# Folding a per-channel scale and shift into the weights and the relu, and normalising all heads at once, in a fused attention and MLP kernel

## The chip, the cores and the metric

The kernel runs on one core of one Trainium2 chip. The metric is the device time of one execution in microseconds (us). A core has five engines that run side by side, each with its own list of instructions in fixed order: TensorE (PE) multiplies matrices out of SBUF into PSUM, VectorE (DVE) and ScalarE (ACT) work elementwise on both memories, GpSimd (POOL) works elementwise on SBUF, and SyncE (SP) issues most of the DMA transfers. They wait for each other through semaphores. The profile counts a weight load of TensorE as an engine of its own, PEld.

## The reference

```python
# attention: batch 4, 8 heads, 768 positions, head size 64; 4 sink keys and a window of 128
scores = q @ k.T / sqrt(64)
keep = is_sink | in_window
a = exp(where(keep, scores, -1e9) - max); a = a / sum(a)
x = (a @ v)                           # laid out as [4, 768, 512]
# residual MLP with affine steps, d_model 512, hidden 2048
a1 = alpha1 * x + beta1
tok = einsum('ts,bsd->btd', w_tok, a1)
u = x + lam * tok
a2 = alpha2 * u + beta2
ch = relu(a2 @ w_ch1) @ w_ch2
out = u + lam * ch
```

Inputs and output are float32; the matrix products are done in float16 with float32 sums.

## The kernel before

The four batches pass one after the other through the same stages, and the attention of the next batch is woven into the MLP of the present one.

Attention. `load_qk`, `trans`: q and k of two heads are cast to float16 and transposed into `qkT`, by TensorE for batches 0 and 1, by the transposing DMA for batches 2 and 3. `scores` computes, for each block j of 128 keys, the scores of the queries in blocks j and j+1, for four heads in one buffer of kind S (two PSUM banks, 1024 columns in all); two of these exist, and one block takes both. ACT takes the exponential into `E`, DVE or POOL masks it. `sinks` does the same for the four sink keys, into `es`. `pv` multiplies `E` with the values, for a block r of 128 queries and a half G of four heads. Each value row has a 1 as its 65th element, so that the 65th column of the result is the sum of the weights. `norm` in `pv` takes the reciprocal of that column and multiplies (L850 and L851). The result of a `pv` stands in a buffer of kind d, one PSUM bank; four of these exist, and the MLP uses them as well. For blocks 2 to 4 of batches 2 and 3 (`EARLY`) the sink part is computed together with the scores of the next block, as two matmuls of 64 rows that run side by side (L711); else it is one matmul of 128 rows for each half (L818).

MLP. On the attention result, POOL and DVE apply alpha1 and beta1 (`xh`; lam is folded into both). `tok` multiplies with the transposed w_tok (L956); DVE adds it to x, which gives u (L963); ACT or POOL casts it to `u16`. u is then transposed: in batch 0 by TensorE (`uTp`, L997), in the others by the transposing DMA (`uTx`, L1015). `affine` applies alpha2 and beta2 to the transposed u, where they are per-partition scalars, in four pieces of 384 columns for each half `chk` of the positions (L980 on ACT, L982 on DVE). `mlp1` computes the hidden layer, fi by fi: four matmuls of 384 columns (L1036), then the relu, on ACT (L1042) or DVE (L1044), into `hT`. For batch 0, `mlp2` does the second product (`ch`, L1221). For batches 1 to 3 it is done by a Strassen scheme with seven products: `h_sums` adds and subtracts quarters of `hT` on DVE (S1 to S4), `w2_sums` those of w_ch2, and `prod` multiplies (P1 to P7, L1153) and adds the results to u (L1166).

What sets the order: nothing runs when it is written. Every piece is added to a plan as a task, with a priority, the engines that can do it with the planner's own cost figure for each, the tasks that it needs, and the buffers that it uses. `Plan.run` simulates the machine and always takes the task that can start first; buffers are given out in that simulation, and where TensorE would stand idle in the first microseconds it puts in multiplications of zeros (`idle`)[...]. The instructions are then written in that order. `TURNS` is a list of seeds by which the priorities are varied before the plan is made. The order is therefore fixed when the kernel is built, and on the chip each engine works through its list.

In the profile, casts and copies have one line for all uses (L356 on ACT, L358 on DVE and POOL).

Of the kernel before, what the change touches and what calls it, by code (L numbers as in the profile page):

```python
# [111 lines left out]
class Plan:  # L112
# [19 lines left out]
    def run(self, prio):  # L132
# [35 lines left out]
        def pick():  # L168
            best = None
            spare = {k: sorted(h for h, x in zip(homes[k], busy[k]) if not x) for k in homes}  # L170
            for r, i in open_:
                at = ready[i]
                if best is not None and at > best[0]:
                    continue
                t = tasks[i]
                asked = {}
                for b in t.uses:
                    if b.home is None:
                        asked[b.kind] = asked.get(b.kind, 0) + 1
                if any(len(spare[k]) < n for k, n in asked.items()):  # L180
                    continue
                at = max([at] + [spare[k][n - 1] for k, n in asked.items()])
                own = None
                for e in t.engs:
                    at_e = max(free[e], at)
                    if e == POOL or (e == DVE and t.port):
                        at_e = max(at_e, port)
                    key = (at_e + FW * t.engs[e], at_e, r, at_e + t.engs[e], i, e)
                    if own is None or key < own:
                        own = key  # L190
                if best is None or own[1:] < best:
                    best = own[1:]
            return best
# [52 lines left out]
    def emit(self, turns):  # L246

        prio = [t.prio for t in self.tasks]
        for seed in turns:
            prio = shuffle(prio, seed)  # L250
        for t, e, start, stop, idle in self.run(prio):
            t.at = (e, start, stop)
            if idle:
                self.fill[1](self.pools["d"][0].tile(
                    [128, 512], FP32, tag=f"d_{idle[0]}", bufs=1, name=f"idle{t.i}"), idle[1])
            for b in t.uses:
                if b.t is None:
                    pool, shape, dtype = self.pools[b.kind]
                    b.t = pool.tile(b.shape or shape, b.dtype or dtype,
                                    tag=f"{b.kind}_{b.home}", bufs=1, name=b.name)  # L260
            t.fn(e)

# [17 lines left out]
def kernel(  # L280
# [51 lines left out]
        "rec": (sb, [P, 4, 1], FP32),  # L332
        "u16": (sb, [P, DM], FP16),
        "uT": (sb, [P, NC, S], FP16),
        "hT": (sb, [P, NF, NTOK], FP16),
# [32 lines left out]
    rsum = const.tile([P, NR], FP32, name="rsum")  # L368
    ab_row = sb.tile([2 * NC, P], FP32, tag="pt_2", bufs=1, name="ab_row")
# [39 lines left out]
    gates = sb.tile([1, 32], FP16, tag="pt_1", bufs=1, name="gates")  # L409
# [7 lines left out]
    TURNS = (13523, 134113, 50022, 128275, 136711, 187603, 125671, 100730, 14946, 163131, 178432, 158827, 183776, 137680, 153375, 26742, 367527, 307353, 376563, 212018, 255075, 397706, 218147, 375675, 393913, 224567, 207692, 352780, 243076, 346008)  # L417
# [164 lines left out]
    EARLY = (2, 3, 4)  # L582
# [107 lines left out]
    def scores(p, b, j, Gs, bias=False):  # L690
# [44 lines left out]
        if b > 1 and j:  # L735
            qk = qk + [done["S", b, j - 1, 0]]
        if early:
            cost += 115
            qk = qk + [done["vs", b, None], done["es", b, 0]]
            more = [es[b]] + [pvb[b, r, G] for G in range(2)]  # L740
        a = add(p, {PE: cost}, mm, qk + [done["bias"]], [o] + [u[3] for u in units] + more, mode="row")
        for G, hps, n, pS, eT in units:
# [8 lines left out]
            if not bias:  # L751
# [12 lines left out]
                if b and j:  # L764
                    c[POOL] = 2 * (150 + n * w * 0.9)
# [43 lines left out]
    def pv(p, b, r, G):  # L809
        early = (b, r, G) in pvb  # L810
        po = pvb[b, r, G] if early else Buf("d", [P, 4, D1], FP32, f"pv{b}_{r}_{G}")
        parts = [(r - 1, P)] * (r > 0) + [(r, 0)]
        Es = [E[b, j, G] for j, _ in parts]

        def mm(e):
            if r >= 2 and not early:
                g = slice(64 * G, 64 * G + 64) if b == 0 else slice(0, P)
                nc.tensor.matmul(  # L818
                    po.t, es[b].t[g, (r - 2) * P : (r - 1) * P], vs[g, 4 * G : 4 * G + 4, :],
                    start=True, stop=False)  # L820
            for hl in range(4):
                h = 4 * G + hl
                i, e_ = hl // 2, hl % 2
                for n, ((j, c), (eT, off)) in enumerate(zip(parts, Es)):
                    nc.tensor.matmul(  # L825
                        po.t[:, hl, :], eT.t[:, e_, off + i, c : c + P], vf[j][:, h, :],
                        start=(r < 2 and n == 0),
                        stop=(n == len(parts) - 1 and (r < 2 or hl == 3)))

        after = [t for j, _ in parts for t in done["E", b, j, G]]  # L830
# [4 lines left out]
        uses = [po] + list(dict.fromkeys(eT for eT, _ in Es))  # L835
        if early:
            after.append(done["S", b, r + 1, 0 if r + 1 < NR - 1 else None])
        elif r >= 2:
            after += [done["vs", b, None if b else G], done["es", b, G if b == 0 else 0]]
            uses.append(es[b])  # L840
        a = add(p, {PE: 245 if early else (130, 245, 355)[min(r, 2)]}, mm, after, uses)
        done["pv", b, r, G] = a
        if G == 0:
            x[b, r] = Buf("x", None, None, f"x{b}_{r}")
            xh[b, r] = Buf("xh", None, None, f"xh{b}_{r}")
# [3 lines left out]
        def norm(e):  # L849
            nc.vector.reciprocal(rec.t, po.t[:, :, D:D1])  # L850
            nc.vector.tensor_mul(  # L851
                bx.t[:, 4 * G : 4 * G + 4, :], po.t[:, :, 0:D], rec.t.to_broadcast([P, 4, D]))

        a = done["x", b, r, G] = add(p + 0.1, {DVE: 640}, norm, [a], [po, rec, bx])
# [10 lines left out]
        elif G == 1:  # L865
# [8 lines left out]
            a = add(p + 0.3, {POOL: 1350}, mul, [a, done["x", b, r, 0], done["la1"]], [bx, bt], port=True)  # L874
# [58 lines left out]
    def cast_w2(p, i):  # L933
        for a in range(4 * i, 4 * i + 4):
            src = wst[f"w2_{a - a % 2}"]
            done["w2", a] = add(
                p, {DVE: 980, POOL: 1400},
# [71 lines left out]
    def uTx(p, b, ti):  # L1009
# [4 lines left out]
        done["uTd", b, ti] = add(  # L1014
# [3 lines left out]
        if ti % 3 < 2:  # L1018
            return
        chk = ti // 3  # L1020
        for c in range(NC):
            o = (c, slice(chk * NTOK, (chk + 1) * NTOK))
            done["uT", b, chk, c] = add(
                p + 0.1 + 0.01 * c, {DVE: 380, ACT: 700},
                lambda e, c=c, o=o: affine(e, bo.t[:, o[0], o[1]], bo.t[:, o[0], o[1]], c),
                [done["uTd", b, 3 * chk + i] for i in range(3)] + [done["ab2"]], [bo])

    def mlp1(p, b, chk, fi):
        if fi == 0:
            hT[b, chk] = Buf("hT", None, None, f"hT{b}_{chk}")  # L1030
        bh, bu = hT[b, chk], uT[b, 0]
        ph = Buf("d", [P, NTOK], FP32, f"h{b}_{chk}_{fi}")

        def mm(e):
            for c in range(NC):
                nc.tensor.matmul(  # L1036
                    ph.t, w1f[:, c, fi * P : (fi + 1) * P],
                    bu.t[:, c, chk * NTOK : (chk + 1) * NTOK], start=(c == 0), stop=(c == NC - 1))

        def relu(e):  # L1040
            if e == ACT:
                nc.scalar.activation(bh.t[:, fi, :], ph.t, AF.Relu)  # L1042
            else:
                nc.vector.tensor_scalar_max(bh.t[:, fi, :], ph.t, 0.0)  # L1044

        a = add(p, {PE: 4 * 161}, mm,
                [done["uT", b, chk, c] for c in range(NC)] + [done["w1", fi // 4]],
                [ph, bu])
        done["h", b, chk, fi] = add(p + 0.1, {ACT: 493, DVE: 556}, relu, [a], [ph, bh])
# [7 lines left out]
    def w2_sums(p):  # L1057

        for g in range(HF // 2):
# [5 lines left out]
            def sub(o, i0, i1, after, n_):  # L1065
# [3 lines left out]
                return add(p + 4 * g + n_, {DVE: 420, POOL: 1400}, f_, after, [bw], port=True)  # L1069
# [8 lines left out]
    def h_sums(p, b, what):  # L1078
# [6 lines left out]
        def s2(g, f):  # L1085
            return own[g].t if own else h0.t[:, f]
# [3 lines left out]
        for g in range(2):  # L1090
# [3 lines left out]
                "S3": lambda e, f=f, g=g: nc.vector.tensor_sub(hs[g].t, h0.t[:, f], h1.t[:, f]),  # L1094
                "S1": lambda e, f=f, k_=k_: nc.vector.tensor_add(h1.t[:, f], h1.t[:, f], h1.t[:, k_]),
                "S2": lambda e, f=f, g=g: nc.vector.tensor_sub(s2(g, f), h1.t[:, f], h0.t[:, f]),
                "S4": lambda e, f=f, k_=k_, g=g: nc.vector.tensor_sub(h0.t[:, k_], h0.t[:, k_], s2(g, f)),
# [12 lines left out]
            done[what, b, g] = add(p + 0.1 * g, {DVE: 880}, made, after, uses, port=True)  # L1110
# [6 lines left out]
    def prod(p, b, what, nt):  # L1117
# [46 lines left out]
        def plus(p, bx, cols, more):  # L1164
# [3 lines left out]
            return add(p, {DVE: 400}, f_, [a, u_] + more, [pc, bx])  # L1168
# [13 lines left out]
        elif what == "P6":  # L1182
# [3 lines left out]
            u = add(p + 0.1, {DVE: 400}, u2, [a, done["read", b, "P1", nt]], [pc, bt])  # L1186
# [9 lines left out]
            done["U12", b, nt] = add(p + 0.3, {POOL: 760, DVE: 400}, ot, [u, done["u16", b, nt]], [bt, top], port=True)  # L1196
# [109 lines left out]
    for b in range(B):  # L1306
# [54 lines left out]
        if b + 1 == STRASSEN[0]:  # L1361
            w2_sums(w0 + ns + PAR["w2s"])
        if b + 1 < B:
# [30 lines left out]
    plan.emit(TURNS)  # L1394
# [35 lines left out]
```

The softmax here doesn't subtract the row's maximum and nothing guards it: scores larger than these inputs give would overflow.

## Time and profile before

| what | value |
| --- | --- |
| time, median of 3 runs | 256.96 us (256.52 to 257.1) |
| span of the profiled execution | 255.3 us |
| TensorE busy | 247.4 us, 97% |
| VectorE busy | 190.0 us, 74% |
| ScalarE busy | 142.6 us, 56% |
| GpSimd busy | 88.3 us, 35% |
| granted TensorE clock | 0.999 |

A busy time is the union of the instructions of an engine; matmuls are pipelined, so a busy TensorE is not one at its peak: a matmul of 384 columns is listed with 326 ns, but in a row they follow each other every 0.16 us. In the groups, a line gives the line of the code, the engine, the operation, what is written and read, shapes, the number of instructions, their busy time, the mean of one in ns, and the idle time of the engine just before them with what ended it. The chain that ended last is followed backwards from the last instruction; in order of time its lines give the start, the length and the work.

### The profile page before, as it was taken

Reading aid. Unit: us, or ns where it says so; the run is one execution under the profiler, and the core shown is the slowest. Engines: PE = TensorE matmul, PEld = TensorE weight load, DVE = VectorE, ACT = ScalarE, POOL = GpSimd, SP = SyncE. Lnnn points to the kernel's source line nnn. Section 1 sums busy time; section 2 is a strip of 40 time slices with the busy share of each in tenths; the row PEclk is TensorE's granted clock in tenths of the full one; section 3 lists DMA queues with packets and bytes.
Section 4 is the critical chain, followed back from the end, with each engine's and each line's share of the span. In section 5 each row is a group of like instructions: output and inputs, shape, how many; then the busy total and the mean of one; then the engine's idle time right before and its main releaser. Section 6 shows DMA issues by size and latency. Waiting matters only on the chain.

```text
span 255.3 us, 5519 instructions
## 1 busy us (share of the span) xinstructions
PE 247.4 (97%) x2174; PEld 160.9 (63%) x2174; DVE 190.0 (74%) x402; ACT 142.6 (56%) x236; POOL 88.3 (35%) x108
## 2 busy tenths in 40 slices
PE   8999998999999999899999999999999999999994
PEld 7754645675555544456678676558668666667883
DVE  6777998696878878578889997877789764136782
ACT  2689845989848035688971225867571125775000
POOL 7409802344445330159653460735310101000000
PEclk9999999999999999999999999999999999999999
DMA  6998999999943998599778689501000156000105
GB/s 202 195 223 292 216 230 392 373 370 218 218 73 115 186 260 190 117 205 220 155 138 182 125 191 251 85 3 21 3 0 3 59 167 146 0 0 3 63 4 185
DMA packets 86130, 38.80 MB, mean 152 GB/s; under 512 B 73540, under 2 KB 80460, under 8 KB 86104
## 3 DMA queue, kind: packets, MB, share of 16 engines
q1 hardware_dynamic: 82320, 35.14, 56.5%
q0 software_dynamic: 3744, 3.28, 8.1%
q8 instruction: 17, 0.28, 0.5%
q14 instruction: 9, 0.07, 0.1%
q10 hardware_dynamic: 40, 0.03, 0.0%
HBM read 29.91 MB, written 6.29 MB: 142 GB/s over the span
## 4 chain that ended last, share of the span: by engine, by line
PE 88%; DMA 4%; DVE 3%; POOL 1%; issue 1%; ACT 1%; POOLq 0%; ACTq 0%
PE h L1036 33%; PE P L1153 21%; PE tok L956 11%; PE ch L1221 8%; PE pv L825 5%; PE S L724 4%; DMA n<-in_q_dram 4%; DVE uT L982 1%; PE S L719 1%; PE tp L614 1%; PE pv L818 1%; POOL n L497 1%; PE wT L916 1%; ACT uT L980 1%; DVE w2f L1068 1%
## 5 line engine op out<-in xcount | busy, mean ns | idle before, releaser
L1036 PE MATMUL h<-uT,w1f 128*128 128x384 f16 x512 | 91.9, 326 | 2.7 <-DVE uT L982 1.3
L1036 PEld LDWEIGHTS <-w1f 128*128 128x128 f16 x512 | 47.3, 98 | 34.5 <-issue 5.5
L1042 ACT ACTIVATE hT<-h 128x384 f16<-128x384 f32 x99 | 48.3, 492 | 26.1 <-PE h L1036 25.6
L1153 PEld LDWEIGHTS <-hT 128*128 128x128 f16 x408 | 39.8, 98 | 6.7
L746 ACT ACTIVATE E<-S 128x1024 f16<-128x1024 f32 (+1 forms) x39 | 37.9, 1001 | 7.5 <-PE S L724 3.7
L869 POOL TENSOR_TENSOR tm<-x,la_b 128x512 f32<-128x512 f32 x18 | 26.2, 1454 | 26.3 <-DVE xh L872 19.1
L956 PE MATMUL tok<-xh,wtokT 128*128 128x512 f16 x144 | 33.4, 379 | 0.0
L356 ACT CAST u<-x 128x512 f16<-128x512 f32 x19 | 11.7, 618 | 31.2 <-DVE x L963 31.1
L1153 PE MATMUL P<-w2f,hT 128*128 128x256 f16 x216 | 25.9, 273 | 0.0
L1166 DVE TENSOR_TENSOR x<-x,P 128x256 f32<-128x256 f32 x45 | 18.3, 418 | 8.2 <-PE P L1153 7.9
L1044 DVE TENSOR_SCALAR hT<-h 128x384 f16<-128x384 f32 x29 | 15.8, 553 | 10.9 <-PE h L1036 10.5
L956 PEld LDWEIGHTS <-wtokT 128*128 128x128 f16 x144 | 14.0, 98 | 14.6
L1221 PE MATMUL ch<-w2f,hT 128*128 128x512 f16 x96 | 23.0, 379 | 0.0
L1153 PE MATMUL P<-w2s,hT 128*128 128x256 f16 x192 | 22.8, 273 | 0.0
L851 DVE TENSOR_TENSOR x<-pv,rec 128x256 f32<-128x256 f32 x48 | 20.4, 424 | 1.7
L358 POOL CAST vfs<-vnat 128x512 f16<-128x512 f32 x18 | 15.0, 840 | 16.2 <-DMA vnat<-in_v_dram 16.0
L963 DVE TENSOR_TENSOR x<-x,tok 128x512 f32<-128x512 f32 x24 | 16.2, 684 | 5.7 <-PE tok L956 5.7
L356 ACT CAST n<-nat 128x768 f16<-128x768 f32 x16 | 13.2, 829 | 10.8 <-DMA nat<-in_q_dram 8.8
L825 PEld LDWEIGHTS <-E 128*128 128x128 f16 x328 | 15.2, 97 | 6.0 <-issue 1.6
L825 PE MATMUL pv<-vfs,E 128*128 128x65 f16 x328 | 17.9, 194 | 0.0
L358 POOL CAST u<-x 128x512 f16<-128x512 f32 x5 | 3.1, 621 | 34.8 <-DVE x L963 21.1
L1221 PEld LDWEIGHTS <-hT 128*128 128x128 f16 x96 | 8.6, 98 | 9.1 <-issue 0.2
(131 smaller groups left out, 327.4 us busy)
## 6 DMA issues: line engine op xcount, KB each, us to landing
out_dram<-x SPq DMA_DIRECT2D x21, 256.0 KB, 2.8
nat<-in_q_dram SPq DMA_DIRECT2D x13, 384.0 KB, 5.3
nat<-in_k_dram SPq DMA_DIRECT2D x13, 384.0 KB, 5.7
vnat<-in_v_dram SPq DMA_DIRECT2D x18, 256.0 KB, 5.2
wst_w<-in_moe_w_ch_dram SPq DMA_DIRECT2D x8, 512.0 KB, 7.4
wtn<-in_moe_w_tok_dram SPq DMA_DIRECT2D x6, 384.0 KB, 4.7
w1f<-in_moe_w_ch_dram POOLq DMA_DIRECT2D x4, 512.0 KB, 11.1
v<-in_v_dram SPq DMA_DIRECT2D x12, 128.0 KB, 6.4
```

The lines of the kernel that those rows point to most:

```text
L356: nc.scalar.copy(o, i)
L358: engine[e].tensor_copy(o, i)
L746: nc.scalar.activation(eT.t, pS.t[:, :, 0 : n * w].rearrange("p e (i w) -> p e i w", i=n), AF.Exp, scale=scale)
L825: nc.tensor.matmul(po.t[:, hl, :], eT.t[:, e_, off + i, c : c + P], vf[j][:, h, :], start=(r < 2 and n == 0), stop=(n == len(parts) - 1 an ...
L851: nc.vector.tensor_mul(bx.t[:, 4 * G : 4 * G + 4, :], po.t[:, :, 0:D], rec.t.to_broadcast([P, 4, D]))
L869: engine[e].tensor_mul(bt.t, bx.t.rearrange("p h d -> p (h d)"), la1_b)
L956: nc.tensor.matmul(pt.t, wtokT[:, si, ti * P : (ti + 1) * P], hs[si].t, start=(si == 0), stop=(si == NR - 1))
L1036: nc.tensor.matmul(ph.t, w1f[:, c, fi * P : (fi + 1) * P], bu.t[:, c, chk * NTOK : (chk + 1) * NTOK], start=(c == 0), stop=(c == NC - 1))
L1042: nc.scalar.activation(bh.t[:, fi, :], ph.t, AF.Relu)
L1153: nc.tensor.matmul(pc.t, hh[:, nt * P : (nt + 1) * P], w(fi), start=(first and n_ == 0), stop=(n_ == HF - 1), skip_group_check=True)
L1166: nc.vector.tensor_add(row(bx)[:, cols], row(bx)[:, cols], pc.t)
L1221: nc.tensor.matmul(pc.t, bh.t[:, fi, nt * P : (nt + 1) * P], w2f[:, fi, :], start=(fi == 0), stop=(fi == NF - 1))
```

## The change

Three changes of the computation, and with them a new order of everything.

1. alpha2 and beta2 are no longer applied to the transposed u of batches 1 to 3. Since (alpha2 * u + beta2) @ w = u @ (alpha2 * w) + beta2 @ w, the first weights are multiplied by alpha2 in place (`fold_w1`, eight pieces of 1024 columns) after batch 0 has used them, and beta2 @ w becomes a bias of the relu. That bias is made in batch 0: two further columns, beta2 and -beta2, stand beside the positions in `uT` (`beta_cols`), pass through the same matmuls and the relu, and their difference is `bw1`, since relu(z) - relu(-z) = z. Batch 0 itself keeps the affine step.
2. For batches 1 to 3, `pv` handles all eight heads of a query block in one buffer of kind S, four heads in each bank, and the normalisation is one reciprocal of 8 columns and one multiplication of 512. Scores of a block j are ordered behind the `pv` of block j - 2. `EARLY` is empty, so the sink part is always the matmul of 128 rows.
3. The order is made from other cost figures and by a second list of seeds, `NUDGES` (628 of them), each of which moves a few priorities or ties a task to one engine.

`uT` rows are 16 elements longer, `hT` rows 2, `rec` holds 8 columns, and the small tile `gates` has a place of its own.

```diff
@@
-        "uT": (sb, [P, NC, S], FP16),
-        "hT": (sb, [P, NF, NTOK], FP16),
+        "uT": (sb, [P, NC, S + 16], FP16),
+        "hT": (sb, [P, NF, NTOK + 2], FP16),
@@
-    gates = sb.tile([1, 32], FP16, tag="pt_1", bufs=1, name="gates")
+    gates = const.tile([1, 32], FP16, name="gates")
@@
-    EARLY = (2, 3, 4)
+    EARLY = ()
@@
+        if b and j > 1:
+            qk = qk + [done["pv", b, j - 2, 1]]
@@
-        po = pvb[b, r, G] if early else Buf("d", [P, 4, D1], FP32, f"pv{b}_{r}_{G}")
+        Gs = (0, 1) if b else (G,)
+        po = Buf("S", None, None, f"pv{b}_{r}") if b else Buf("d", [P, 4, D1], FP32, f"pv{b}_{r}_{G}")
@@
         def norm(e):
-            nc.vector.reciprocal(rec.t, po.t[:, :, D:D1])
+            if b:
+                pp = po.t[:, :, 0 : 4 * D1].rearrange("p g (h d) -> p g h d", h=4)
+                rr = rec.t.rearrange("p (g h) o -> p g h o", g=2)
+                nc.vector.reciprocal(rr, pp[:, :, :, D:D1])
+                nc.vector.tensor_mul(
+                    bx.t.rearrange("p (g h) d -> p g h d", g=2), pp[:, :, :, 0:D], rr.to_broadcast([P, 2, 4, D]))
+                return
...
@@
-        for c in range(NC):
-            o = (c, slice(chk * NTOK, (chk + 1) * NTOK))
-            done["uT", b, chk, c] = add(
-                p + 0.1 + 0.01 * c, {DVE: 380, ACT: 700},
-                lambda e, c=c, o=o: affine(e, bo.t[:, o[0], o[1]], bo.t[:, o[0], o[1]], c),
-                [done["uTd", b, 3 * chk + i] for i in range(3)] + [done["ab2"]], [bo])
+    def beta_cols(p):
...
+                nc.vector.tensor_scalar(
+                    out=bo.t[:, :, S + n_], in0=beta2_c, scalar1=sign, scalar2=None, op0=ALU.mult)
...
+    def fold_w1(p):
...
+            lambda e: engine[e].tensor_sub(bw1, bh.t[:, :, NTOK], bh.t[:, :, NTOK + 1]),
...
+                    if e == ACT:
+                        nc.scalar.activation(w, w, AF.Copy, scale=al)
...
@@
-                nc.scalar.activation(bh.t[:, fi, :], ph.t, AF.Relu)
+                nc.scalar.activation(o, ph.t, AF.Relu, **({"bias": be} if b else {}))
+            elif b:
+                nc.vector.tensor_scalar(out=o, in0=ph.t, scalar1=be, scalar2=0.0, op0=ALU.add, op1=ALU.max)
@@
-    plan.emit(TURNS)
+    plan.emit(TURNS, NUDGES)
```

## The prediction

> **What bounds the kernel now.** I read the page's first four parts, then the groups of instructions with shapes kept apart, then the chain that ended last in order of time. From the page:
>
> ```profile
> span 255.3 us, 5519 instructions
> PE 247.4 (97%) x2174; PEld 160.9 (63%) x2174; DVE 190.0 (74%) x402; ACT 142.6 (56%) x236; POOL 88.3 (35%) x108
> PE   8999998999999999899999999999999999999994
> PE 88%; DMA 4%; DVE 3%; POOL 1%; issue 1%; ACT 1%; POOLq 0%; ACTq 0%
> ```
>
> TensorE is busy in every slice and carries 88% of the chain. A faster VectorE or ScalarE is worth something only where TensorE stops for it. The chain in order of time (start, length, what) shows the three places after the start where it does:
>
> ```profile
> 38.63 0.35 PE uTp L997 x6
> 39.06 0.68 ACT uT L980
> 39.76 0.87 DVE uT L982 x2
> 40.66 0.68 ACT uT L980
> 41.38 2.27 PE h L1036 x13
> ...
> 99.94 1.26 DVE x L963 x2
> 101.80 0.27 ACT uT L980
> 102.07 0.71 DMA qkT<-n
> 102.78 0.59 DVE uT L982
> ...
> 177.92 1.90 DVE uT L982 x2
> 179.82 0.34 DVE x L1166
> 180.20 0.82 PE h L1036 x4
> ```
>
> All three pass through the affine step `uT`, which the change takes away for batches 1 to 3. How large are they? The steady step is 0.1625 us for one h matmul (32 in 5.20 us), so 0.65 for a group of four.
> - First: the transposes end at 39.13; up to 41.38 only 3 h matmuls (0.49) were issued. Lost: 2.25 - 0.49 = 1.76 us.
> - Second: tok's last 18 matmuls start at 97.71 and step 0.215, so they end at 101.6. The next 12 h matmuls (1.95) are done only when S starts at 105.25. Lost: 3.65 - 1.95 = 1.7 us.
> - Third: eight P matmuls from 178.79 end at 179.66; h comes at 180.20, because the sum `x` that frees its PSUM buffer stood behind two stretched `uT` on DVE. Lost: about 0.5 us.
> One small one more: 12 h matmuls from 110.29 reach to 112.50, 0.26 us too long. Together some 4.2 us. Counting all TensorE work after 38.5 us by its steady steps, with about 0.11 for each return from a row-split score group, leaves 4 to 5 us of 213.5 unexplained; so there is no fifth large gap.
>
> The costs that the change touches, from the groups (busy us, mean ns, then idle time before):
>
> ```profile
> L1042 ACT ACTIVATE hT<-h 128x384 f16<-128x384 f32 x99 | 48.3, 492 | 26.1 <-PE h L1036 25.6
> L851 DVE TENSOR_TENSOR x<-pv,rec 128x256 f32<-128x256 f32 x48 | 20.4, 424 | 1.7
> L850 DVE RECIPROCAL rec<-pv 128x4 f32<-128x4 f32 x48 | 8.6, 178 | 7.6 <-PE pv L825 7.2
> L982 DVE TENSOR_SCALAR uT<-uT,ab 128x384 f16<-128x384 f16 x17 | 7.7, 502 | 3.9 <-DMA uT<-u 3.9
> L980 ACT ACTIVATE uT<-uT,ab 128x384 f16<-128x384 f16 x7 | 4.7, 699 | 0.0
> L980 ACT ACTIVATE uT<-uTp,ab 128x384 f16<-128x384 f16 x6 | 3.9, 672 | 2.0 <-PE uTp L997 1.0 <-DVE uT L982 0.9
> L711 PE MATMUL pv<-vs,es 64*128 64x260 f16 x12 | 1.7, 282 | 0.0
> ```
>
> **What the Trainium skill says.** "ScalarE: Activation LUTs", section What ACT_TABLE_LOAD costs: each [128,1] pointer operand of an ACTIVATE adds about 93 ns. The trace agrees: the affine step from PSUM has two pointers and takes 672, the relu of the same 384 columns has none and takes 492; half the difference is 90. "PSUM — Partial Sum Buffer", section PSUM bank collisions raise a hardware error: two engines must not touch one bank and quadrant at once. This fits the turns that ACT and DVE take at 39.06, 39.76 and 40.66 over tiles of one bank each. "VectorE: DVE Perf Modes", section What auto-detection actually checks: two elements per cycle need 16-bit tensors with step 1. The hT sums run at 956 to 1057 ns for 1536 elements here; a row pitch of 386 instead of 384 keeps both conditions, so I leave their cost as it is. "TensorEngine Tiling (Array Packing)", section Key Properties: different row tiles run in parallel, and a change of mode drains. The trace has both: two L711 matmuls take 0.12 us together (117.74 to 117.86), and the h group after a score group takes 0.76 instead of 0.65.
>
> **The change part by part.**
> Affine of batches 1 to 3. Removed: 17 on DVE, 7.7 us busy (most take about 376 ns, the longest 1424), and 7 on ACT, 4.7 us. At the second gap h then waits for the last transposing DMA alone. In before, that wait is filled by 4 ch and 18 tok matmuls; in the new order by tok1_4, S2_0, tok1_3, tok1_5, the sink scores and S2_1: 3 x 1.29 + 2 x 0.65 + 0.33 = 5.5 us behind tok1_2. From the end of tok1_2 (96.85) to the landing of its transposes took 4.3 us in before (issue of the third at about 98.8, 2.4 to land). So the gap closes: -1.5, leaving 0.2 for its last wait. The third gap falls with the DVE stretch that made it: -0.4. The small one: -0.2, since h no longer shares its PSUM buffers with pv.
> First gap. Batch 0 keeps its affine step, but the order is new: both engines begin on the second transposed tile, DVE first (0.47), then ACT (0.67) while DVE does the two others. 0.2 + 0.47 + 0.67 + 0.1 = 1.44 after the first tile instead of 2.7 (38.98 to 41.38, with the turns), but DVE now does three of the four and h takes the last one later: I take -0.4.
> Fold. Eight [128 x 1024] multiplications, all on ACT in the new order, between the scores of batch 1: near 1023 (the exp row of the same size) plus one pointer, so 1.1 us each, 9 us. ACT is busy 11.7 of 25 us between 68 and 93, and nothing needs the weights before about 100. Cost 0. The two sign columns add 64 x 2 columns, 0.05 us: nothing.
> Relu with bias. 77 of the relus of batches 1 to 3 are on ACT: 492 + 90 = 582 each, 6.9 us more, against 4.7 saved. In the stretch with nothing but h, one comes each 0.65 us, so 0.58 still keeps up. Among exps (two of 1.02 per score step) ACT had 22.5 of 27 us busy at 103 to 130 and stays near 85%; four PSUM buffers, now without pv, absorb a relu that is 0.1 to 0.5 late. Charged below. The DVE relu's cost with a pointer isn't in the trace; the affine from PSUM, two pointers, took 471, so I take 553 unchanged (up to 90 more as the upper end: 23 x 0.09 = 2 us of an engine with slack).
> Normalisation. 36 pairs of 178 + 424 leave, 21.7 us; 18 pairs of about 182 + 684 (tok's add of 512 columns from PSUM) come, 15.6. DVE gains 6 us, which is off the chain: 0.
> Values in the two-bank buffer. Scores take both S buffers, pv now needs one of them, and S(j) is also ordered behind pv(j-2). Behind a waiting pv or S on TensorE stand h matmuls, and behind those everything. I walked batch 1's hand-over with the durations above: S2_2 needs the second exp of S2_1 and pv2_0's norm, which are done about 1 us before it; S2_3 has 0.7 us, S2_4 0.5, pv2_3 0.3, S2_5 0.4. All fit, but with tenths to spare. Five or six such places in each of three batches: +0.4, between 0 and 2.5.
> Sink part. EARLY empty: 6 row-split pairs at 0.12 become 6 x 2 full matmuls at 0.11: +0.6 with what follows each.
> Start. The fifth cast load (the q of pair 3, from which the chain begins: issued 6.03, landed 15.40) becomes the fourth, one 0.72 us issue earlier, and the five mask selects (0.52 + 3 x 0.28 + 0.39 = 1.75) move behind the sixth load. But the DMA engines are near full from 2 us on, and the filler matmuls rise from 106 to 116. -0.6, between 0 and -1.4.
> Sum: -1.5 - 0.4 - 0.2 - 0.4 - 0.6 + 0.6 + 0.4 = -2.1; 256.96 - 2.1 = 254.9.
>
> **The rivals.**
> A. New waits on the S buffers and the slower relu take back what was won, and more. For: the margins above are 0.3 to 1 us, ACT is at 85%, and the cost table of the new code still counts 493 for a relu with bias; 18 places at 0.15 us make 2.7. Also all eight transposes of batch 2's q and k (1.24 to 1.5 us each on the SP queue) now stand before batch 1's uT; in before two stand behind. If these are 2 us late, TensorE stops at S2_0. Against: pv left the four single buffers, so h has more room. Either gives 254.9 + 2.7 = 257.6: slower.
> B. The gaps close and the start shortens by all its 1.4, with no new waits: 254.9 - 0.8 - 0.4 - 1.0 (the first gap to 0.36) = 252.7.
> C. The affine was hidden in effect, because the DMA landing ends at the same time: only 0.6 of the second gap goes (the last affine) and the rest is used up by the sink part: 256.9, no change.
>
> **How the numbers follow.** Forecast 0.54, A 0.20, B 0.18, C 0.08. Faster: forecast and B with a little of C lost, 0.73; same 0.07; slower 0.20. The range takes in B and A: 252.4 to 257.8; beyond are a start that gains more and waits above 2.5 us.
>
> **What would show it.** Right: no uT group on DVE or ACT after 50 us; h following S2_1 without idle near 103; DVE busy near 177 (190 - 7.7 - 6), ACT near 154 (142.6 - 4.7 + 9 + 6.9); relus at 580 on ACT; 18 pairs near 0.87. Wrong: TensorE idle before S or pv released by the exp line or the normalisation, h released by a relu, or a stop at S2_0 released by the transposing DMA.

## The result, and the profile after

The changed kernel takes 259.64 us (259.27 to 259.96), the kernel before 256.77 beside it: a ratio of 1.0111, 95% interval 1.0092 to 1.0130. The forecast of 254.9 was wrong in sign, and its range ended at 257.8. A ratio uses the fast executions alone and need not be the quotient of the two medians; in two of the runs below (258.50 and 258.75 us) a few slow executions stand in the time and not in the ratio.

The page of the changed kernel: span, busy times, and the chain by engine.

```profile
span 258.2 us, 5481 instructions
PE 249.7 (97%) x2184; PEld 162.6 (63%) x2184; DVE 187.8 (73%) x356; ACT 147.8 (57%) x227; POOL 95.4 (37%) x110
PE 90%; DMA 3%; DVE 3%; ACT 1%; issue 1%; SPq 0%
```

TensorE still carries the time. So the loss is to be looked for where TensorE does other work than before, and where it stops. The waits of TensorE (total us, times, longest):

```profile
PE uTp L1068 <- ACT uT L1051: 1.5, 1, 1.5
PE idle L400 <- DVE warm L427: 1.1, 1, 1.1
PE h L1135 <- DMA uT<-u: 0.7, 1, 0.7
PE h L1135 <- DVE uT L1053: 0.6, 1, 0.6
PE tp L667 <- DVE n L409: 0.5, 1, 0.5
PE h L1135 <- ACT hT L1142: 0.4, 1, 0.4
PE S L777 <- DMA qkT<-n: 0.2, 1, 0.2
```

The first, the longest, is new, and it lies in batch 0, whose computation the change leaves alone but for the two sign columns. The chain in order of time (start, length, what) shows how it comes about, and what became of the gap ahead of batch 1's h:

```profile
40.26 0.35 PE uTp L1068 x6
40.63 0.37 DVE uT L1053
41.10 0.31 issue
41.41 0.48 DVE uT L1053
41.93 0.66 PE h L1135 x3
42.65 0.44 issue
43.09 4.04 DVE w2f L1009 x3
47.13 0.40 DVE uT L1053
47.55 0.68 ACT uT L1051
48.28 0.49 PE uTp L1068 x6
...
104.92 2.44 DMA uT<-u
107.50 5.36 PE h L1135 x32
```

What the reader is to see, in order:
- The start. The uTp transposes of batch 0 begin at 40.09 us, 1.6 later than before (38.47). No wait of TensorE is listed between 17 and 40 us in either kernel; but 22 filler matmuls, which compute nothing, now stand on the chain from 17.5 us on, where the kernel before has 12 from 16.9 on. The point moves between executions too: with the changed kernel's start untouched it lies at 39.45 to 40.09 in three traces of this case, with the old start at 38.06 to 38.60 in eight, if beta2's columns don't hold it up (see the fold, below).
- The first gap is about 0.75 us shorter than before; both engines begin on other tiles.
- The stall. VectorE has three multiplications of w_ch2 (`w2f`) ahead of the affine of the next uTp tile. They take 4.04 us; six of the same took 3.69 in the kernel before (lines below). The affine comes at 47.05, ScalarE's half behind it, and TensorE waits 1.46 us for the buffer: +1.6.
- When tok of batch 1 begins (96.92 us after 92.96), the kernel is 3.1 us behind, counted without four ch matmuls (0.86 us) that before come later.
- The gap ahead of batch 1's h: no affine any more, but h waits 0.74 us for the landing of uT's transposes, and S 0.21 for qkT's. Lost there: some 1.2 us after 1.7 before. The third gap of before (180 us) is gone, -0.5; a wait for a relu at 115 us is new, +0.4; the sink's part of the values is made of full matmuls now. From here to the end this nearly cancels: the last addition ends 2.9 us later than before.

These multiplications on VectorE and GpSimd, first in the kernel before:

```profile
40.77 1.27 POOL L938 TENSOR_TENSOR w2f<-wst_w,lam_b 128x512 f16<-128x512 f32 x1 [0.65 <-DMA wst_w<-in_moe_w_ch_dram]
41.13 1.46 DVE L938 TENSOR_TENSOR w2f<-wst_w,lam_b 128x512 f16<-128x512 f32 x1
42.98 3.69 DVE L938 TENSOR_TENSOR w2f<-wst_w,lam_b 128x512 f16<-128x512 f32 x6
```

and then in the changed one, beside VectorE's three at 43.09:

```profile
43.43 3.15 POOL L1009 TENSOR_TENSOR w2f<-wst_w,lam_b 128x512 f16<-128x512 f32 x2 [0.59 <-DMA wst_w<-in_moe_w_ch_dram]
```

The kernel before had the same effect once, at 41.13: one multiplication beside GpSimd's took 1.46 us, and the six without GpSimd 0.62 each.

The groups that answer to the prices of the prediction (busy us, mean ns, idle time before):

```profile
L1142 ACT ACTIVATE hT<-h,bw 128x384 f16<-128x384 f32 x76 | 43.9, 582 | 23.1 <-PE h L1135 15.3 <-PE P L1260 4.8
L1144 DVE TENSOR_SCALAR hT<-h,bw 128x384 f16<-128x384 f32 x20 | 12.1, 613 | 11.2 <-PE h L1135 11.1
L1115 ACT ACTIVATE w1f<-w1f,ab 128x1024 f16<-128x1024 f16 x8 | 8.9, 1149 | 0.0
L1009 DVE TENSOR_TENSOR w2f<-wst_w,lam_b 128x512 f16<-128x512 f32 x13 | 12.8, 1030 | 0.0
L1009 POOL TENSOR_TENSOR w2f<-wst_w,lam_b 128x512 f16<-128x512 f32 x3 | 4.4, 1490 | 0.6 <-DMA wst_w<-in_moe_w_ch_dram 0.6
```

The prices of the new operations were nearly right (the multiplication of 512 in the normalisation: 692 ns where 684 was taken). What wasn't priced is in the last two rows: w2f's multiplication, which the change doesn't touch, took 735 ns on VectorE before and takes 1030 now.

### The profile page after: what moved, and what is told of

Same layout as the page of the kernel before. It is cut to its first block, busy times and chain, and to the rows that moved or that the text cites. A ratio compares the mean times of both kernels' runs of the same rounds, so it can differ in the third digit from the quotient of the medians.

```text
span 258.2 us, 5481 instructions
## 1 busy us (share of the span) xinstructions
PE 249.7 (97%) x2184; PEld 162.6 (63%) x2184; DVE 187.8 (73%) x356; ACT 147.8 (57%) x227; POOL 95.4 (37%) x110
## 4 chain that ended last, share of the span: by engine, by line
PE 90%; DMA 3%; DVE 3%; ACT 1%; issue 1%; SPq 0%
PE h L1135 31%; PE P L1260 21%; PE tok L1027 11%; PE ch L1328 8%; PE pv L888 5%; PE S L777 4%; DMA nat<-in_k_dram 2%; PE pv L881 2%; DVE w2f L1009 2%; PE S L772 2%; PE idle L400 1%; PE tp L667 1%; PE tp L664 1%; DMA uT<-u 1%; PE wT L987 1%
## 5 line engine op out<-in xcount | busy, mean ns | idle before, releaser
L1135 PE MATMUL h<-uT,w1f 128*128 128x384 f16 (+1 forms) x512 | 90.6, 326 | 1.9 <-DMA uT<-u 0.7
L1135 PEld LDWEIGHTS <-w1f 128*128 128x128 f16 x512 | 48.1, 98 | 33.6 <-issue 4.4
L1142 ACT ACTIVATE hT<-h,bw 128x384 f16<-128x384 f32 x76 | 43.9, 582 | 23.1 <-PE h L1135 15.3
L940 POOL TENSOR_TENSOR tm<-x,la_b 128x512 f32<-128x512 f32 x18 | 24.7, 1371 | 36.1 <-DVE x L916 20.9
L1027 PE MATMUL tok<-xh,wtokT 128*128 128x512 f16 x144 | 32.2, 379 | 0.0
L1144 DVE TENSOR_SCALAR hT<-h,bw 128x384 f16<-128x384 f32 x20 | 12.1, 613 | 11.2 <-PE h L1135 11.1
L407 ACT CAST n<-nat 128x768 f16<-128x768 f32 x15 | 12.2, 832 | 12.3 <-DMA nat<-in_q_dram 11.8
L888 PE MATMUL pv<-vfs,E 128*128 128x65 f16 x328 | 16.8, 193 | 0.0
L816 DVE TENSOR_TENSOR E<-E,maskn 128x1024 f16<-128x1024 f16 x21 | 15.8, 758 | 0.6 <-ACT E L801 0.5
L1201 DVE TENSOR_TENSOR hS<-hT,hT 128x1536 f16<-128x1536 f16 x6 | 5.7, 950 | 11.9 <-ACT hT L1142 11.9
```

The lines of the kernel that those rows point to most:

```text
L407: nc.scalar.copy(o, i)
L816: nc.vector.tensor_mul(ev, ev, m.to_broadcast(list(ev.shape)))
L888: nc.tensor.matmul(bank(G)[:, hl, :], eT.t[:, e_, off + i, c : c + P], vf[j][:, h, :], start=(r < 2 and n == 0), stop=(n == len(parts) - 1 ...
L940: engine[e].tensor_mul(bt.t, bx.t.rearrange("p h d -> p (h d)"), la1_b)
L1027: nc.tensor.matmul(pt.t, wtokT[:, si, ti * P : (ti + 1) * P], hs[si].t, start=(si == 0), stop=(si == NR - 1))
L1135: nc.tensor.matmul(ph.t, w1f[:, c, fi * P : (fi + 1) * P], bu.t[:, c, chk * NTOK : chk * NTOK + n_], start=(c == 0), stop=(c == NC - 1))
```

## The experiments

Each order was written out as a list (task, engine, buffer number) that stands in place of the planner's result, and single entries of the list were moved, so that nothing else moves with them. In the diffs below, a line is an engine's queue; SyncE's is SP in the profile.

Theory 1: the stall at 46 us is VectorE and GpSimd in each other's way. Theory 2: the start is 1.6 us late because of its new order. Theory 3: the fold is good, and the loss is the order's alone. Rival to all: the slower relu and the new waits on the S buffers cost what was lost.

### GpSimd's multiplications taken away from VectorE's

```diff
 VectorE: w2f, w2f, w2f, uT, relu, relu, uT, relu ...
-GpSimd:  w2f, w2f (wst_w2_4, wst_w2_0), w2s
+VectorE: ... relu, w2f (wst_w2_0) ... w2f (wst_w2_4)
+GpSimd:  w2s
```

> The changed kernel in its own order, except that GpSimd's second and third multiplication of w_ch2 by lambda (the two at 43.4 to 46.6 us) go to VectorE some us later, so that VectorE's three at 43.09 us have nothing of GpSimd's beside them. Nothing is left out. Theory 1 (the stall at 46.65 us exists because VectorE and GpSimd slow each other down: 1.35 us for each of VectorE's three where it took 0.62 alone): the three take about 2.0 us instead of 4.04, the affine after them starts at about 45.6, TensorE's wait of 1.5 us before the uTp transposes at 48.3 goes, and the kernel takes 258.1 us, ratio to before about 1.005. Rival (the stall is slack that a later wait absorbs, or the three multiplications are slow for another reason): 259.6 us, ratio 1.011, and in the latter case the three still take 4 us.

Measured: 258.99 us, ratio 1.0071 (1.0051 to 1.0092). VectorE's timeline, and below it TensorE's (start, length, engine, line, operation, names, shapes, count):

```profile
42.96 1.89 DVE L1021 TENSOR_TENSOR w2f<-wst_w,lam_b 128x512 f16<-128x512 f32 x3
45.42 0.48 DVE L1065 TENSOR_SCALAR uT<-uTp,ab 128x384 f16<-128x384 f16 x1 [0.58 <-PE uTp L1080]
```

```profile
46.66 0.49 PE L1080 MATMUL uTp<-iden,u 128*128 128x128 f16 x6
```

The same three instructions on the same engine take 1.89 us instead of 4.04 when GpSimd does nothing beside them, and the 1.46 us stall is gone. This is the strongest result here: nothing else was changed near them. "SBUF — State Buffer" in the Trainium skill, section Who interferes with whom, says that a VectorE instruction with two SBUF inputs contends with a GpSimd instruction that reads SBUF, and that the ports which the two share are an exclusive lock. The runs agree in kind: three at 0.63 and two of GpSimd's at 1.27 one after another would be 4.4 us, and 4.04 were measured, so the turns are nearly strict ones. Of the 1.6 us, 0.6 by the medians and 1.0 by the ratios reaches the end: a relu behind the multiplications that VectorE took over lets h wait 0.69 us at 53.87, and w2s, now later, lets h wait 0.57 us at 106 us.

### The affine ahead of the third multiplication

```diff
-VectorE: w2f, w2f, w2f, uT, relu
+VectorE: w2f, w2f, uT, w2f, relu
```

> The changed kernel in its own order, except that VectorE's third multiplication of w_ch2 by lambda at 43.09 us stands behind the affine of the uT tile rather than ahead of it. GpSimd stays as it is. Theory 1 (VectorE's queue ahead of the affine makes TensorE's stall at 46.65 us): the affine starts about 1.35 us earlier, at 45.7, TensorE waits 0.1 to 0.3 us instead of 1.5, and the kernel takes 258.2 to 258.5 us, ratio about 1.006. Rival (TensorE waits there for ScalarE or a transfer that has its own reason): the wait stays within 0.3 us of 1.5 and the time is 259.6 us.

Measured: 258.83 us, ratio 1.0079 (1.0060 to 1.0098). TensorE doesn't wait at these transposes any more; h just behind them waits 0.60 us for a relu, which now stands behind the third multiplication. So the queue ahead of the affine makes the stall, and the contention makes the queue long; either cure gives 0.6 to 1.0 us.

### The start in the old order

```diff
-all queues up to the first uTp: order of the changed kernel
+all queues up to the first uTp: order of the kernel before
```

> The changed kernel, but every task ahead of the first uTp transposes (some 190 of 1093) stands in the order and on the engine that the kernel before has; all later tasks keep the order of the changed kernel. Nothing is left out. Theory 2 (the new order of the start costs 1.6 us: TensorE does waits and filler matmuls early and so reaches uTp at 40.09 instead of 38.47): uTp starts at 38.4 to 38.8 and the kernel takes about 258.0 us, ratio 1.005. Rival (the start is not what the later stages wait for, since the weights' transfers and the VectorE queue set them): uTp starts early but the gain is gone by 50 us, and the time is 259.4 to 259.8 us.

Measured: 258.02 us, ratio 1.0048 (1.0031 to 1.0065), 1.6 us less than the changed kernel, as theory 2 said. The trace shows only part of this. It is of the longest of the six executions (259.05 us); uTp starts at 39.55, 0.54 earlier than in the changed kernel and not at the expected 38.4 to 38.8, since beta2's two small instructions hold up VectorE (see the fold, below); the stall of 1.46 us is still there. With them at a better place the same start gives 38.53 and 38.60 in the last runs of this section. h then waits 0.80 us for uT.

### The changed kernel without its late fillers

```diff
-TensorE: idle x3 (17.5 us), idle x8 (18.3), idle x3 (27.3), idle x8 (28.4)
```

> The changed kernel in its own order, without its last 22 filler matmuls (3, 8, 3 and 8 of 128x128 at 17.5, 18.3, 27.3 and 28.4 us), which compute nothing of the output. Theory 2 in the form that the fillers themselves cost the time of the start: up to 22 times 54 ns, 1.2 us, 258.4 us, ratio 1.0065. Rival (they stand where TensorE would wait anyway, for the bias, the cast and the sinks, so the loss of the start is the order of the tasks): 259.2 to 259.7 us, ratio 1.010.

Measured: 258.50 us, ratio 1.0060 (1.0039 to 1.0081), 1.3 us less than the changed kernel by the ratios. uTp starts at 39.12, 1.0 us earlier. But this isn't the price of the fillers. The changed kernel ahead of the first of them and after the last:

```profile
16.15 0.53 PE L664 MATMUL tp<-iden,n 128*64 128x128 f16 x12
31.64 0.51 PE L987 MATMUL wT<-iden,wt 128*128 128x128 f16 x6
```

and this run at the same two places:

```profile
15.55 0.53 PE L676 MATMUL tp<-iden,n 128*64 128x128 f16 x12
30.67 0.51 PE L999 MATMUL wT<-iden,wt 128*128 128x128 f16 x6
```

It is 0.60 us ahead before anything was left out, since its second group of transposes begins at 7.92 us after 8.54, and 0.97 behind the last filler. So 22 fillers, which make 1.2 us (eight in a row take 0.45), cost 0.4 us in these two traces; for the rest TensorE waits in their place (0.32 us for a cast at 18.00, for one). The stall was 0.38 us here instead of 1.46, though nothing was moved near it: GpSimd's two multiplications, which wait for a load, begin 1.07 us behind VectorE's three instead of 0.34, and the three take 2.96 us. The gain is therefore mixed, and the rival, that the fillers stand where TensorE would wait anyway, holds here for about two thirds of their time.

### The fold alone, in the old order

The kernel before, each queue as it was, with `alpha2` into w_ch1, beta2 as the relu's bias, and no affine in batches 1 to 3:

```diff
-VectorE, ScalarE: affine on uT, 24 tasks
+VectorE: beta2's columns (at 23 us); bw1 (at 80 us)
+ScalarE: w1f[c] *= alpha2, x8 (at 73 to 93 us)
```

> The kernel before with its own order on every engine, and of the change only the fold: alpha2 multiplied into w_ch1 by eight ScalarE instructions placed into ScalarE's idle time at 73 to 93 us, beta2 as the bias of relu in batches 1 to 3, no affine on uT there; the values of the heads are normalised four by four as before, and the sink's early matmuls stay. Nothing is left out. Theory 3 (the fold itself is good and the loss of the changed kernel is its new order): the gap ahead of the h matmuls of batch 1, 1.7 us in the kernel before, falls below 0.5 us, the third gap of 0.4 goes, and the kernel takes 254.8 to 255.6 us, ratio about 0.994. Rival (the slower relu, 582 ns for 490 on ScalarE and 613 for 552 on VectorE, costs more than the affine did, so the fold is itself slower): 257 us or more, ratio over 1.001.

Measured: 256.93 us, ratio 1.0002 (0.9992 to 1.0012). Neither theory: the fold isn't slower, but its gain was missing. TensorE's timeline of this run:

```profile
102.40 2.11 PE L1077 MATMUL h<-uT,w1f 128*128 128x384 f16 x12
104.44 0.50 PE L737 MATMUL S<-qkT 64*128 64x256 f16 x6
105.84 0.28 PE L737 MATMUL S<-qkT 64*128 64x256 f16 x2 [0.90 <-DMA qkT<-n]
```

The gap ahead of h has closed: no idle time stands in the first line. In the third line TensorE waits 0.90 us for the transposes that bring qkT. They had been late in the kernel before as well, but h was later still and hid it. And TensorE came 0.65 us late to tok. VectorE and GpSimd at beta2's columns:

```profile
23.51 1.59 DVE L1038 TENSOR_SCALAR uT<-ab 128x4 f16<-128x4 f32 x2
23.57 1.42 POOL L873 TENSOR_TENSOR xh<-x,la_b 128x256 f16<-128x256 f32 x2
```

The two writes of four columns take 0.17 us each elsewhere; here one of them lasts 1.52 us and ends with GpSimd's two products (24.99), and a cast behind it on VectorE comes late, for which TensorE waits 0.89 us. The run with the old start has the same 1.52 at the same place. No wait of VectorE is listed there, so it doesn't look like a wait for a buffer, as the next expectation has it. It looks like the stall's contention once more; no run takes GpSimd's products away there, so this stays argued. Two further runs separate the two losses:

```diff
-VectorE: beta2's columns at 23 us
+VectorE: beta2's columns behind the first affines, at 39 us
```

> The fold alone of the run before (256.93 us, ratio 1.000), with one thing moved: the two small VectorE instructions that write beta2 into uT's spare columns stood at about 23 us, where they waited for the buffer of v and held up the cast behind them (TensorE waited 0.89 us for it at 26 us); here they follow the first affines at 39 us. Theory 3a (0.65 us of the fold's gain went there by my placing): 256.2 to 256.4 us, ratio 0.9975, and the wait of 0.9 us for qkT at 105 us stays. Rival (the start has slack): 256.9 us.

Measured: 256.24 us, ratio 0.9976 (0.9963 to 0.9989). The start gives its 0.65 back, and the two writes take 0.17 us each.

```diff
-SyncE:   store x, qkT<-n, qkT<-n, uT<-u x3, loads of v
+SyncE:   qkT<-n, qkT<-n, store x, uT<-u x3, loads of v
-TensorE: h x12, S, sk, h x16
+TensorE: h x16, S, sk, h x12
```

> As the run with the fold alone and beta late, and two moves at the start of batch 1's h: the store of x ahead of the last two qkT transposes on the SyncE queue goes behind them, and one group of four h matmuls goes ahead of the scores of batch 2 on TensorE. Theory 3b (the gap ahead of h hid a transfer: with the affine gone the scores wait 0.9 us for qkT instead, which is why the fold alone gained nothing): the wait for qkT goes, and the time is 255.2 to 255.6 us, ratio 0.9945, which is faster than the kernel before and the changed kernel. Rival (what is gained there is lost at a later wait): 256.2 us, as without the two moves.

Measured: 255.84 us, ratio 0.9956 (0.9941 to 0.9971). The wait for qkT is gone, but the expected 255.2 to 255.6 wasn't quite reached. Its waits show why:

```profile
PE pv L838 <- POOL E L699: 1.2, 2, 1.1
```

At 112 us the values wait for a mask on GpSimd, which stands behind a cast there, which waits for v, whose load stands behind uT's transposes on SyncE. One move more:

```diff
-SyncE: qkT<-n, qkT<-n, store x, uT<-u x3, load v, load v ...
+SyncE: qkT<-n, qkT<-n, store x, load v, uT<-u x3, load v ...
```

> As the fold with beta late and the two moves (255.84 us, ratio 0.9956), and the first load of v for batch 2 goes ahead of the three uT transposes on the SyncE queue: in that run TensorE waited 1.08 us at 112 us for a mask on GpSimd which stood behind the cast of that v. Theory 3c (what the fold saves is paid again at the next thing that SyncE's queue brings late; each such wait is a move away): the wait of 1.08 us goes, 254.7 to 255.1 us, ratio 0.9915. Rival (uT's three transposes, now 0.55 us later, or another wait take it): 255.6 to 256 us.

Measured: 254.95 us, ratio 0.9934 (0.9917 to 0.9950), faster than both kernels. Each of the last two steps is hardly clear of its interval; the two together, from 256.24, are. All the waits of TensorE that are left:

```profile
PE idle L361 <- DVE warm L388: 1.1, 1, 1.1
PE h L1077 <- ACT uT L993: 0.9, 2, 0.5
PE h L1077 <- DVE uT L995: 0.2, 1, 0.2
PE pv L838 <- POOL E L699: 0.2, 1, 0.2
```

One at the very start, those for the affine of batch 0, which the change leaves alone, and 0.2 us.

Does the slower relu cost anything? The same as the run with beta2's columns late, with the bias left out of the relu:

```diff
-activation(o, ph, Relu, bias=be)
+activation(o, ph, Relu)
```

> The fold alone with beta late (256.24 us, ratio 0.9976) without the bias in relu: beta2's part of h is left out in batches 1 to 3, so relu costs what it cost before the fold, 490 ns on ScalarE and 552 on VectorE, in place of 582 and 613. If the slower relu lies beside other work: 256.0 to 256.3 us, ratio 0.997. If TensorE waits for it (58 and 19 of them in batches 1 to 3, about 6 us of engine time in all): 255 us or less, ratio 0.993.

Measured: 256.04 us, ratio 0.9971 (0.9960 to 0.9983), against 0.9976 with it: no difference that these intervals can tell. Some 8 us more of ScalarE's and VectorE's time (77 x 90 ns and 19 x 60) are hidden. This rival falls for the old order.

Two more, on the order with v early. Without its last 12 fillers:

```diff
-TensorE: idle x1 (16.9 us), idle x7 (17.6), idle x4 (28.2)
```

> As the fold with v early, without its last 12 filler matmuls (1, 7 and 4 of 128x128 at 16.9, 17.6 and 28.2 us), which compute nothing of the output. Leaving out 22 of them gained 1.1 us in the changed kernel; at the same price 12 gain 0.6: 254.1 to 254.5 us, ratio 0.990. If these stand where TensorE waits anyway: no difference to the run with v early.

254.93 us, ratio 0.9933 (0.9916 to 0.9949): nothing. In this order leaving them out gives nothing that can be told. And with the sink's part as full matmuls:

```diff
-    EARLY = (2, 3, 4)
+    EARLY = ()
```

> As the fold with v early (254.95 us, ratio 0.9934), with EARLY empty as in the whole change: the sink's part of the values of batches 2 and 3 is no longer issued as row-split pairs inside the scores (12 matmuls, two in 0.12 us) but as full matmuls ahead of each values group. The prediction's term for it is +0.6 us: 255.5 us, ratio 0.9957. If the later, longer matmuls lie beside a wait of TensorE: 255.0 us. If they delay a normalisation that frees a buffer: over 256 us.

255.66 us, ratio 0.9950 (0.9936 to 0.9964), 0.4 us more by the ratios; the two intervals overlap, so a cost of the sink's part isn't shown by this run, and one above 1 us isn't likely.

### Do the losses of the changed kernel add up?

```diff
 old start, with beta2's columns behind the first affines
-VectorE: w2f, w2f, w2f, uT
+VectorE: w2f, w2f, uT, w2f
-SyncE:   store x, store x, uT<-u x3
+SyncE:   uT<-u x3, store x, store x
```

> The whole change, with three losses of its order undone together: the start in the order of the kernel before (beta2's columns written after the first affines), VectorE's third multiplication of w_ch2 behind the affine, and two stores of x behind the three uT transposes at 101 us on the SyncE queue. If the losses add (start 1.6 to 2.2, stall 1.0 to 1.5, uT's landing 0.5 to 0.7 us): 255.4 to 256.5 us, ratio 0.996 to 0.999. If they hide one another: 257.3 to 258 us, no better than the start alone (258.0).

Measured: 258.42 us, ratio 1.0042 (1.0021 to 1.0064). That is worse than either expectation and no better than the old start alone (258.02): the gains don't add. TensorE's timeline:

```profile
48.24 3.43 PE L1147 MATMUL h<-uT,w1f 128*128 128x386 f16 x20 [0.87 <-ACT uT L1063]
...
101.40 0.40 PE L789 MATMUL S<-qkT 64*128 64x256 f16 x4 [0.56 <-DMA qkT<-n]
114.78 4.71 PE L1147 MATMUL h<-uT,w1f 128*128 128x384 f16 x28 [1.36 <-ACT E L813]
```

The stall wasn't undone in this execution, the longest of the nine: VectorE's first multiplication waits 1.50 us for its load, and TensorE 0.30 us at the transposes (45.55) and 0.87 at h behind them. At 114.78, h doesn't read E. The second half of uT, which it reads, had its last two transposes behind loads of v on SyncE. Moved ahead:

```diff
-SyncE: uT<-u, load v, load v, uT<-u, uT<-u
+SyncE: uT<-u, uT<-u, load v, uT<-u, load v
```

> As the whole change with its three losses undone (258.42 us, ratio 1.0042), and the last two uT transposes of batch 1 no longer stand behind two loads of v on the SyncE queue. In that run TensorE waited 1.36 us at 114.8 us at the first h matmuls that read them; the profile put it down to ScalarE's exponential, which they do not read. Theory 3d (it is the transposes' landing): the wait goes, 257.0 to 257.3 us, ratio 0.999. Rival (it is ScalarE's backlog of relus and exponentials): still over 1 us there, 258.4 us.

Measured: 260.66 us, ratio 1.0148 (1.0114 to 1.0181), worse. The longest wait of TensorE:

```profile
PE pv L900 <- POOL vfs L421: 2.3, 1, 2.3
```

The wait of 1.36 became 0.85, at 113.13, and now names the transposes: the reading of the landing was right in kind. But v came late in turn, 2.3 us. A wait was moved along one queue and grew.

Last, the changed kernel's own order with the fillers, GpSimd's multiplications and the two stores mended, and nothing of the old order:

```diff
-TensorE: the last 22 fillers
-GpSimd:  w2f, w2f
+VectorE: ... w2f ... w2f
-SyncE:   store x, store x, uT<-u x3
+SyncE:   uT<-u x3, store x, store x
```

> The whole change in its own order with three of the losses undone, and nothing taken from the order of the kernel before: the last 22 filler matmuls left out, GpSimd's two multiplications of w_ch2 moved to VectorE some us later, the two stores of x behind the three uT transposes. Single gains were 1.1 us (fillers) and 0.65 (multiplications). If start and stall are separate losses: 257.2 to 257.9 us, ratio 1.003, a rest of about 0.6 us over the kernel before, which would be the sink's part. If SyncE's queue takes back what is gained, as with the old start: 258.3 us or more.

Measured: 258.75 us, ratio 1.0060 (1.0030 to 1.0090), no better than without the fillers alone. Its SyncE queue and TensorE:

```profile
89.46 0.57 SPq L1354 DMA_DIRECT2D out_dram<-x  x1
90.09 0.42 SPq L573 DMA_DIRECT2D nat<-in_q_dram  x1
90.56 10.32 SPq L695 DMA_TRANSPOSE qkT<-n  x6
```

```profile
95.84 5.34 PE L1039 MATMUL tok<-xh,wtokT 128*128 128x512 f16 x24
101.12 0.39 PE L789 MATMUL S<-qkT 64*128 64x256 f16 x4
102.55 0.40 PE L789 MATMUL S<-qkT 64*128 64x256 f16 x4 [1.03 <-DMA qkT<-n]
```

TensorE reaches tok 1.1 us sooner than in the changed kernel (96.92), but the last part of S comes at 102.55 instead of 102.79. Six transposes stand in a row on SyncE: the first is listed with 3.65 us, the others with 1.3 each, so that the last is issued at 99.59 and lands 2.9 us later, when S goes on. Batch 1's beginning is paced there. Why the first takes so long isn't shown; a load of q, behind a store, was issued just ahead of it (90.09).

What wasn't tried: the common normalisation by itself. In the new order the values of batch 1 stand where all four d buffers hold sums of `ch`, so they can't be split back into d buffers at these places; in the old order they would have found no free S buffer. Its share is known only from the trace of the changed kernel, where TensorE has no wait for an exponential or a normalisation that frees an S buffer.

## Why the prediction was wrong

Three steps of the sum failed: the start had the wrong sign, no term stood for VectorE's queue ahead of the second pair of uTp tiles, and a gap was booked at its full length.

- "Start ... -0.6, between 0 and -1.4": this step failed first. It read two issues that move forward, and dismissed the ten more fillers because the DMA engines are near full. Measured +1.6, and the old start in its place returns 1.6 us. What in the new order makes it late is only in part known: leaving the late fillers out returns 1.3 by the ratios, of which the traces put some 0.4 down to the fillers. The count of 106 and 116 was in the prediction, but not where they stand.
- "First gap ... -0.4": right in direction for the first tile (about -0.75). (The 2.7 in this term is 2.4 by the times given with it, 38.98 to 41.38.) But I walked the second pair of tiles no further, and there stood the stall: +1.6 at that place, of which 0.6 to 1.0 reaches the end. No term of the sum had it. The profile of the kernel before had its price, 1.46 us for one multiplication beside GpSimd's, and I didn't look there. The diff showed the costs of w2f changed (980 to 850 on VectorE, 1400 to 1450 on GpSimd), which says that the order had been looked for again; who stands beside whom then has to be read anew, even where nothing is computed differently. The planner does count the two engines as taking turns, with GpSimd's two behind VectorE's three, at 45.2 and 46.6 us of the plan; nothing in the program holds GpSimd back, and on the chip it began at 43.43.
- "So the gap closes: -1.5": measured about -0.5 in the changed kernel, and -0.2 for the fold alone in the old order (from tok to the sink's scores 7.91 us after 8.09). The gap did close, but the next thing was late too: qkT by 0.9 us in the old order, uT and qkT by 0.95 together in the new one. This is what rival C described, which got 0.08, and rival A's remark on the eight transposes ahead of uT. I had compared uT's landing with the work that lies beside it, but took its issue as of before (98.8), while six transposes and two stores put it to 102.31.
- "Third gap -0.4": gone, about -0.5. "Small one -0.2": nothing to be told apart.
- "Fold: cost 0": right. 1149 ns each instead of 1.1, all hidden; the run with the fold and three moves is faster than before by 1.7 us.
- "Relu with bias": 582 on ScalarE as forecast, and hidden in the old order. On VectorE 613 where I took 553, within the bound that was given.
- "Values in the two-bank buffer +0.4": no wait on the S buffers; one relu at 115 us, 0.4 us. The walk through the margins held.
- "Sink part +0.6": 0.4 by a run of its own, whose interval leaves room for 0.6 and for nothing.
- The rivals: A ended on the right side, 2 us short, and for the most part by another mechanism. Of the signs that it named, two showed, both small (h released by a relu, 0.43 us; S by the transposing DMA, 0.21). The loads came out otherwise, VectorE 187.8 us where 177 was forecast and ScalarE 147.8 where 154 was, as the new order gives VectorE more relus (36 after 29) and masks; TensorE is the bound, so this is no loss by itself. The chance of 0.20 for slower was too low because every case in the table was about what the change computes, and none about what its new order does to the rest.

Of the 2.9 us the profile names: start +1.6, first gap -0.75, stall +1.6, some 0.6 spread over batch 0 up to tok that I didn't trace, gap ahead of h -0.5, relu +0.4, third gap -0.5, sink +0.4 (an estimate from the two ratios): 2.85. These are differences of two traces, each of which moves by some tenths at the start alone. That they are places and not independent costs, the runs suggest: undone together they gave 1.3 to 1.8 us by the ratios, not 3, though in the traced one of the two the stall had come back in part.

## What to carry to other kernels

When a change comes with a new order of all work, the part that isn't computed differently has to be read like new code: walk each queue ahead of the critical instructions, and ask which other engine works on the same memory beside it. A gap on the bounding engine is worth no more than the lateness of the next thing that this engine will wait for; look that one up before the gap is booked as a gain. And where several mended waits don't add up, look for one queue on which all their transfers stand: here SyncE, on which two moves, with one on TensorE, were worth 1.1 us by the ratios (0.9976 to 0.9934).

## What was new of the hardware

- VectorE and GpSimd, both on products of two float32 tensors in SBUF (128x512, written as float16): VectorE's took 1.35 us each beside GpSimd's and 0.63 alone; GpSimd's 1.58 and 1.27.
- A VectorE write of 128x4 in SBUF lasted 1.52 us beside two GpSimd products of 1.42 us together, in two runs, and 0.17 elsewhere.
- A bias pointer in VectorE's relu from PSUM costs some 60 ns (613 after 552), in ScalarE's 90 (582 after 492).
- A scale by a pointer on ScalarE, from SBUF to SBUF in float16, takes 1149 ns for 1024 columns, 126 more than the exponential of as many from PSUM.
